# Loading a weight half ahead of the fourth head pair, and swapping a chunk of q on VectorE

## The chip, the cores and the metric

The kernel runs on one core of one Trainium2 chip. Its time is the device time of one launch in microseconds (us). The engines are TensorE (PE, with its weight loads as PEld), VectorE (DVE), ScalarE (ACT), GpSimd (POOL) and SyncE (SP), which here issues nearly all transfers.

## The reference

```python
def _attn_ref(q, k, v):                      # 4 batches, 8 heads, 576 positions, head size 64
    scores = scale * np.matmul(q, k.transpose(0, 1, 3, 2))
    gamma = 1.0 - 2.0 ** (-5.0 - np.arange(H))
    Dmat = np.where(rel >= 0, gamma[:, None, None] ** rel[None, :, :], 0.0)
    return np.matmul(scores * Dmat[None, :, :, :], v)

def _moe_ref(x, w_in, w_out):                # 2304 tokens, 512 -> 2048 -> 512
    h = x @ w_in
    g = h * np.clip(h + 3.0, 0.0, 6.0) / 6.0
    return g @ w_out

def _moe2_ref(x, w_in, w_out, g_ln):         # 512 -> 1024 -> 512
    h = x @ w_in
    solu = h * softmax(h)
    ln = (solu - mean(solu)) / np.sqrt(var(solu) + 1e-06) * g_ln
    return ln @ w_out
```

The output is `_moe2_ref(_moe_ref(_attn_ref(q, k, v)))`, with the heads of a token laid side by side as its 512 features. The inputs are float32; the weights of the two MLPs are float64, and reach the chip as pairs of 32-bit words.

## The kernel before

**Retention.** The 32 heads are taken as 16 pairs; a pair lies with one head on partitions 0 to 63 and the other on 64 to 127. The 576 positions of a pair are cut into four chunks of 128 and one of 64. Within a chunk the scores are computed and masked; what earlier chunks give is carried in a state of 64x64 per head, decayed from chunk to chunk. `attention()` (L533) is a generator with three steps for each pair `pr`. Step 0 puts out `scores(pr)`, `last_scores(pr)` and `from_states(pr - 1)`; step 1 the loads of pair `pr + 3`, `chunk_states(pr)` and `prep(pr + 1)`; step 2 `values(pr - 1)`. The matmuls of all these and most of ACT's evacuations are held in the order of the program (`keep_in_program_order`), and so are SP's weight loads. All else, VectorE's work and the loads of the pairs among it, is ordered by a planner that simulates the program.

**What an engine does for a pair.** ACT scales v by a decay (`prep`, L436, three instructions, tile `v` with two buffers), and evacuates the two score banks (`st`, L455). POOL masks the scores (L456). DVE multiplies the last chunk's scores by a mask (L501), makes the four states (`chunk_states`, L470 one copy and L476 four scaled sums, two of them on 64 partitions) and evacuates the pair's result (`xa`, L527). ACT and POOL then split `xa` into two words (L260, L261). There is one buffer each for the score banks and for `xp`, in which the result is summed, so the scores of a pair wait for `st` of the pair before, and `from_states(pr)` waits for `xa` of pair `pr - 1`.

**Why q's chunk 3 is swapped.** The fourth state lies with its heads exchanged (L468, L472), so `from_states` needs chunk 3 of q with its heads exchanged too: it reads `rq[:, S:]` (L517). The host has put that exchanged copy behind q's 576 columns in HBM (L1019). For pairs 0 to 2 (`EARLY`) the kernel loads it as a transfer of its own, behind the pair's other four (L425); for the later pairs it is part of the load of q (L417), which is then 704 columns wide.

**The weights.** The first MLP's weights are prepared beside the retention. Each half is loaded as 512 KB of raw words (`wraw`, two buffers, L119). `value` makes float32 from them with two ACT instructions (`wz` L139, `wt` L144) and two of DVE (L147, L148). `words` then splits the value into a high word (ACT, L153) and a low word (DVE or POOL, L158). In the loop at L591 the first raw half is loaded after step 2 of pair 0, the second after step 2 of pair 1. `begin` (the value) runs after step 1 of even pairs from pair 2 on, and `step` (the words) after step 2 of odd pairs from pair 3 on. From pair 4 on (`A_FROM`) each step 2 also puts out a share of the first MLP's matmuls (`mlp_h`, L272), which fill the TensorE time beside the retention.

**Transfers.** Eight semaphores take turns for SP's transfers, so that an issue waits for the landing of the transfer eight places before it.

After the retention come the rest of the first MLP (L272, L297), and the second MLP with the norm and the output (L71 in the profile, since a helper records these).

```python
        for h in range(2):
            keep(se.activation(out=st[h], in_=sp[h], func=ACTF.Copy, ...))       # L455
...
        ve.tensor_copy(out=state[:, 0], in_=up[:, 0])                            # L470
...
            (1, state[:, 0], rq[:, CHUNKS[1]]), (3, state[:, 2], rq[:, S:]),     # L517
...
        ve.tensor_tensor(out=xa, in0=xp[:, 128:704], in1=tab_sb[p], op=ALU.mult) # L527
```

Of the kernel before, what the change touches and what calls it, by code (L numbers as in the profile page):

```python
# [18 lines left out]
B, H, S, D = 4, 8, 576, 64  # L19
# [15 lines left out]
NX = 8  # L35
STEPS_B = ((6, 20, 42, 50, 58, 66), (6, 20, 42, 50, 58, 66), (4, 12, 20, 28))
W_FROM = 2
A_FROM = 4
AHEAD = 2
WRAW = 2  # L40
# [34 lines left out]
def retention_hardswish_solu_kernel(ctx, tc, kt, qt, kn, vt, w1, w2i, w2o, gln, decay, place, out):  # L75


    nc = tc.nc
    ve, se, ge, te, sy = nc.vector, nc.scalar, nc.gpsimd, nc.tensor, nc.sync
# [84 lines left out]
    def w_half(home, i, name):  # L164

        if home == "w":
            return p0.tile([128, 2, 512], F32R, tag="wi" if i == 0 else "wo", bufs=FA, name=name)
        return pb.tile([128, 2, 512], F32R, tag="wbi" if i == 0 else "wbo", bufs=4, name=name)

    def w1_halves(ffs, home, order):  # L170

        for k, i in order:
            ff = ffs[k]
            if (ff, 1 - i) not in w1t and home == "wb":
                for j in range(2):
                    w1t[ff, j] = w_half(home, j, f"w1_{ff}_{j}")

            def tile_of(ff=ff, i=i):
                if home == "w":
                    w1t[ff, i] = w_half(home, i, f"w1_{ff}_{i}")  # L180
                return w1t[ff, i]

            yield w1[ff][:, i * 1024:(i + 1) * 1024], lambda ws, raw, tile_of=tile_of: (
                ws.words(tile_of(), ws.begun.pop(), pin=True) if ws.begun else ws.words(tile_of(), ws.value(raw))
            )

    def in_first(n):
        return [(k, i) for i in range(2) for k in range(n)]

    def in_turn(n, ahead):  # L190

        return sorted(in_first(n), key=lambda ki: (ki[0] + ahead * ki[1], -ki[1]))
# [196 lines left out]
    raws, vs, sts, sts4, states, us, xps = {}, {}, {}, {}, {}, {}, {}  # L389
    HEADS, ALL = [slice(0, 64), slice(64, 128)], slice(0, 128)  # L390
    CHUNKS = [slice(128 * c, min(128 * c + 128, S)) for c in range(NV)]
# [7 lines left out]
    def mm_a(*args, **kw):  # L399
        keep(nc.tensor.matmul(*args, **kw))  # L400

    def load_pair(pr):

        if pr >= NPAIR:
            return
        early = pr < EARLY
        if early:
            tag = "wi" if pr < 2 else "g"
            rk, rq, rn = [p0.tile([128, n], F32, tag=tag, bufs=FA, name=f"raw{pr}_{i}")
                          for i, n in enumerate((S, S + 128, 512))]  # L410
        else:
            rk = pa.tile([128, S], F32, tag="rk", bufs=3, name=f"rk{pr}")
            rq = pa.tile([128, S + 128], F32, tag="rq", bufs=4, name=f"rq{pr}")
            rn = pa.tile([128, 512], F32, tag="rn", bufs=3, name=f"rn{pr}")
        nc.sync.dma_start(out=rk, in_=kt[pr])
        n = S if early else S + 128
        nc.sync.dma_start(out=rq[:, :n], in_=qt[pr][:, :n])  # L417
        if early:
            rv = p0.tile([128, 9, D], F32, tag="g", bufs=FA, name=f"rv{pr}")
        else:  # L420
            rv = pa.tile([128, 9, D], F32, tag="rv", bufs=3, name=f"rv{pr}")
        nc.sync.dma_start(out=rv, in_=vt[pr])
        nc.sync.dma_start(out=rn, in_=kn[pr])
        if early:
            nc.sync.dma_start(out=rq[:, n:], in_=qt[pr][:, n:])  # L425
        raws[pr] = rk, rq, rn.rearrange("p (c d) -> p c d", d=128), rv

    def prep(pr):
# [13 lines left out]
    def scores(pr):  # L442

        sp = [ps_a.tile([128, 512], F32, tag=f"s{h}", bufs=1, name=f"s{pr}_{h}") for h in range(2)]
        st = sts[pr] = [pa.tile([128, 512], F32, tag=f"st{h}", bufs=2, name=f"st{pr}_{h}") for h in range(2)]
        k, q, _, _ = raws[pr]
        for c in range(4):
            for o in range(2):
                for h in range(2):
                    mm_a(  # L450
                        sp[h][HEADS[o], CHUNKS[c]], k[HEADS[h], 128 * c + 64 * o:128 * c + 64 * o + 64],
                        q[HEADS[h], CHUNKS[c]], start=(c == 0), stop=(c == 3),
                    )
        for h in range(2):
            keep(se.activation(out=st[h], in_=sp[h], func=ACTF.Copy, scale=GAMMA[2 * (pr % NP) + h] ** -128))  # L455
            keep(ge.affine_select(  # L456
                out=st[h], in_=st[h], compare_op=ALU.is_ge, fill=0.0,
                base=0, pattern=[[0, 4], [1, 128]], channel_multiplier=-1,
            ))

    def chunk_states(pr):

        rn, v = raws[pr][2], vs[pr]
        up = ps_a.tile([128, 4, 64], F32, tag="u", bufs=1, name=f"u{pr}")
        state = states[pr] = pa.tile([128, 4, 64], F32, tag="state", bufs=2, name=f"state{pr}")
        for c in range(4):
            for h in range(2):
                o = HEADS[1 - h if c == 3 else h]  # L468
                mm_a(up[o, c], rn[:, c, HEADS[h]], v[:, 4 * h + c], start=(c == 0), stop=(c == 3))
        ve.tensor_copy(out=state[:, 0], in_=up[:, 0])  # L470
        for c, to, at in (
            (1, ((ALL, ALL),), H + pr % NP), (2, tuple(zip(HEADS, HEADS[::-1])), H + pr % NP),  # L472
            (3, ((ALL, ALL),), H + 2 * NP + pr % NP),
        ):
            for i, o in to:
                ve.scalar_tensor_tensor(  # L476
                    out=state[o, c], in0=state[i, c - 1], scalar=decay_sb[i, at:at + 1], in1=up[i, c],
                    op0=ALU.mult, op1=ALU.add,
                )

    def places():

        pp = mm_tile([128, NP * 128], "place")
        mm_a(pp, place_row[:, :128], place_row[:, 128:], start=True, stop=True)
        keep(se.activation(out=place_sb.rearrange("p a b -> p (a b)"), in_=pp, func=ACTF.Copy))
# [9 lines left out]
    def last_scores(pr):  # L495
        zp = ps_a.tile([128, 64], F32, tag="z", bufs=1, name=f"z{pr}")
        st4 = sts4[pr] = pa.tile([128, 64], F32, tag="st4", bufs=2, name=f"st4{pr}")
        k, q, _, _ = raws[pr]
        for h in range(2):
            mm_a(zp[HEADS[h]], k[HEADS[h], CHUNKS[4]], q[HEADS[h], CHUNKS[4]], start=True, stop=True)  # L500
        ve.tensor_tensor(out=st4, in0=zp, in1=mask4[:, pr % NP], op=ALU.mult)  # L501
# [31 lines left out]
    def attention():  # L533

        for pr in range(NPAIR + 1):
            if pr < NPAIR:
                scores(pr)
                last_scores(pr)
            if pr:
                from_states(pr - 1)  # L540
            if pr < NPAIR:
                idle_mm(N_IDLE.get(pr, 0))
                if pr == 0:
                    places()
            yield pr
            if pr < NPAIR:
                load_pair(pr + EARLY)
                chunk_states(pr)
                prep(pr + 1)
                if pr < NP:  # L550
                    widen(pr)
            yield pr
            if pr:
                values(pr - 1)
            yield pr
            if pr == 1:
                tc.keep_in_program_order(nc.sync.dma_start(out=gln_sb, in_=gln))
# [11 lines left out]
    def idle_mm(n):  # L569
        for _ in range(n):  # L570
            mm_a(warm, idle[:, :128], idle[:, 128:], start=True, stop=True)

    idle_mm(N_WARM)
    for pr in range(EARLY):
        load_pair(pr)
# [3 lines left out]
    for h in range(2):  # L579
        ge.affine_select(  # L580
            out=mask4[HEADS[h]], in_=mask4[HEADS[h]], compare_op=ALU.is_ge, fill=0.0,
# [6 lines left out]
    g = [{}, {}]  # L588
    hs = mlp_hs(0, FIRST, g[0], g_a, True)
    wq = Weights(w1_halves(FIRST, "w", in_first(FA)), True, 2)  # L590
    for s, pr in enumerate(attention()):  # L591
        if pr < W_FROM and s % 3 == 2:
            wq.load_to(pr + 1)
        if pr >= W_FROM and pr % 2 == 0 and s % 3 == 1:
            wq.begin()
        if pr > W_FROM and pr % 2 == 1 and s % 3 == 2:
            wq.step()
        if pr >= A_FROM and s % 3 == 2:
            for _ in range(2):
                next(hs, None)  # L600
# [13 lines left out]
    wq = Weights(w1_halves(FB[:4], "wb", in_turn(4, 3)), False)  # L614
# [65 lines left out]
    wq = None  # L680
    for i, j in enumerate(mlp_by_ff(4, list(range(FA)), g_a, evac_partial, ps_c, first_b, X2_LAG * NP)):
        if j == 0 and wq is None:
            wq = Weights(w1_halves(FB[4:], "w", in_turn(len(FB) - 4, 1)), False)
# [230 lines left out]
    ve, se, ge, te, sy = (Pinned(tc, e) for e in (ve, se, ge, te, sy))  # L914
# [145 lines left out]
```

## Time and profile before

| | us |
|---|---|
| median of 3 runs | 649.73 (648.87 to 650.22) |
| the profiled execution, its own time | 648.45 |
| its span | 646.7 |
| PE busy in the span | 640.3 (99%) |
| PEld | 533.3 (82%) |
| ACT | 370.7 (57%) |
| DVE | 332.5 (51%) |
| POOL | 325.3 (50%) |

The granted TensorE clock is full in all 40 slices of the span. A busy share is a mean over stages that differ; matmuls overlap their weight loads and their ends are modelled, so idle time of PE is told apart from slow work by the waits and the chain. In the rows, times are in us from the start of the span; a bracket `[0.71 <-DMA x]` tells how long the engine sat idle before the instruction, and what ended that.

### The profile page before, as it was taken

How to read it: one execution, taken by the hardware profiler on the slowest of the kernel's cores; microseconds unless marked ns; L12 is line 12 of the kernel's file. 1: busy time of each engine (PE TensorE's matmuls, PEld its weight loads, DVE VectorE, ACT ScalarE, POOL GpSimd, SP SyncE). 2: the span in 40 equal slices, each digit the busy share in tenths (PEclk: the TensorE clock that was granted, in tenths of full speed). 3: DMA queues.
4: the chain of work that ended last, by engine and by line, in shares of the span. 5: the costliest groups of instructions: out<-in, count | busy, mean ns of one | idle time of the engine just before them, and what ended most of it. 6: DMA issues, size and time to landing. Idle time of an engine off the chain costs nothing.

```text
span 646.7 us, 11131 instructions
## 1 busy us (share of the span) xinstructions
PE 640.3 (99%) x4178; PEld 533.3 (82%) x4178; DVE 332.5 (51%) x618; ACT 370.7 (57%) x653; POOL 325.3 (50%) x342
## 2 busy tenths in 40 slices
PE   8999999999999999999999999999999999999998
PEld 5788888888889888888888888889988888888887
DVE  3777635244205363253565336112688877878750
ACT  5888837464426575164366247115377768787582
POOL 4778834122312434145044024516279899999353
PEclk9999999999999999999999999999999999999999
DMA  9999416296025252557864655239695334434441
GB/s 323 392 393 378 151 54 242 94 320 218 16 68 191 62 179 90 153 172 292 289 214 152 223 181 178 94 129 367 224 254 122 81 99 111 118 81 98 75 105 67
DMA packets 80459, 114.01 MB, mean 176 GB/s; under 512 B 42642, under 2 KB 47890, under 8 KB 80404
## 3 DMA queue, kind: packets, MB, share of 16 engines
q1 hardware_dynamic: 80256, 113.27, 54.6%
q8 instruction: 33, 0.54, 0.3%
q14 instruction: 22, 0.18, 0.1%
q10 hardware_dynamic: 148, 0.02, 0.0%
HBM read 71.85 MB, written 31.98 MB: 161 GB/s over the span
## 4 chain that ended last, share of the span: by engine, by line
PE 96%; DMA 2%; ACT 1%; DVE 0%; issue 0%; SPq 0%; ACTq 0%
PE h L272 31%; PE x L297 20%; PE o L71 15%; PE h L71 13%; PE acc L297 8%; PE xp L400 3%; PE x L71 2%; PE s L400 2%; PE u L400 1%; DMA wraw<-in_w_dram 1%; DMA raw<-in_qt_dram 1%; DMA raw<-in_kn_dram 1%; DVE w L158 0%; PE z L400 0%; ACT st L455 0%
## 5 line engine op out<-in xcount | busy, mean ns | idle before, releaser
L291 POOL TENSOR_TENSOR g<-gf,g 128x512 fp32r<-128x512 f32 (+1 forms) x78 | 96.0, 1231 | 216.0 <-ACT g L290 205.0
L297 PE MATMUL x<-g,w 128*128 128x512 f32 x576 | 132.0, 389 | 0.0
L272 PE MATMUL h<-xb,w 128*128 128x512 f32 (+1 forms) x600 | 129.7, 360 | 0.2 <-DVE w L158 0.2
L297 PEld LDWEIGHTS x<-g,w 128*128 128x128 f32 x576 | 108.1, 188 | 22.4
L272 PEld LDWEIGHTS h<-xb,w 128*128 128x128 f32 x600 | 98.5, 189 | 17.9 <-issue 1.9
L285 DVE SCALAR_TENSOR_TENSOR gf<-r,h 128x512 f32<-128x512 f32 (+1 forms) x80 | 50.5, 633 | 119.9 <-ACT r L284 106.3
L71 PE MATMUL o<-w,lt 128*128 128x512 f32 (+1 forms) x456 | 103.1, 378 | 0.0
L71 PEld LDWEIGHTS o<-w,lt 128*128 128x128 f32 x456 | 82.4, 188 | 16.3 <-POOL lt L71 0.4
L284 ACT ACTIVATE r<-h,half 128x512 f32<-128x512 f32 (+1 forms) x80 | 50.7, 637 | 64.6 <-PE h L272 64.6
L272 PE MATMUL h<-xB,w 128*128 128x512 f32 x360 | 82.4, 389 | 0.0
L272 PEld LDWEIGHTS h<-xB,w 128*128 128x128 f32 x360 | 67.6, 188 | 14.0
L290 ACT ACTIVATE g<-gf 128x512 fp32r<-128x512 f32 (+1 forms) x78 | 46.1, 591 | 43.5 <-DVE gf L285 38.1
L71 POOL TENSOR_TENSOR lt<-lT,lt 128x512 fp32r<-128x512 f32 x36 | 60.9, 1708 | 13.9 <-ACT lt L71 12.7
L297 PE MATMUL acc<-g,w 128*128 128x512 f32 (+1 forms) x264 | 61.9, 361 | 0.0
L71 ACT ACTIVATE e<-h,stat 128x1024 f32<-128x1024 f32 x36 | 41.3, 1148 | 34.1 <-DVE stat L71 34.1
L147 DVE TENSOR_SCALAR wz<-wz 128x512 int32<-128x512 int32 x44 | 29.6, 672 | 48.6 <-ACT wz L139 48.6
L297 PEld LDWEIGHTS acc<-g,w 128*128 128x128 f32 x264 | 46.9, 188 | 8.8
L71 PE MATMUL h<-w2t,xt 128*128 128x512 f32 x216 | 53.5, 389 | 0.0
L71 PEld LDWEIGHTS h<-w2t,xt 128*128 128x128 f32 x216 | 40.3, 188 | 8.2
L71 PE MATMUL h<-w2b,xt 128*128 128x512 f32 x162 | 39.9, 390 | 0.1
L139 ACT ACTIVATE wz<-wraw 128x512 f32<-128x512 f32 x44 | 29.3, 665 | 18.1 <-DMA wraw<-in_w_dram 9.4
L71 PEld LDWEIGHTS h<-w2b,xt 128*128 128x128 f32 x162 | 30.1, 188 | 6.6 <-issue 0.5
(114 smaller groups left out, 839.6 us busy)
## 6 DMA issues: line engine op xcount, KB each, us to landing
wraw<-in_w_dram SPq DMA_DIRECT2D x32, 512.0 KB, 5.5
xs<-xb SPq DMA_DIRECT2D x12, 512.0 KB, 7.2
xB<-xs SPq DMA_DIRECT2D x12, 512.0 KB, 6.2
rv<-in_vt_dram SPq DMA_DIRECT2D x16, 288.0 KB, 6.0
x2l<-x2s SPq DMA_DIRECT2D x18, 256.0 KB, 4.1
x2f<-x2o SPq DMA_DIRECT2D x18, 256.0 KB, 3.6
x2r<-x2f SPq DMA_DIRECT2D x9, 512.0 KB, 3.9
rq<-in_qt_dram SPq DMA_DIRECT2D x13, 352.0 KB, 6.2
```

Source lines behind the costliest of these rows:

```text
L71: return lambda *args, **kw: self.keep(op(*args, **kw))
L139: first = se.activation(out=z.bitcast(F32), in_=raw[:, :, 1].bitcast(F32), func=ACTF.Prelu, scale=2.0 ** -112, alpha=2.0 ** 32)
L147: ve.tensor_scalar(out=z, in0=z, scalar1=3, scalar2=None, op0=ALU.logical_shift_left)
L272: mm = nc.tensor.matmul(hp, w1t[ff, 0][:, a, c], xb[t, p][:, b, :n], start=(p == 0 and i == 0), stop=(p == NP - 1 and i == 2),)
L284: se.activation(out=r, in_=hp, func=ACTF.Relu, scale=1.0 / 6.0, bias=half)
L285: ve.scalar_tensor_tensor(out=gf, in0=r, scalar=1.0, in1=hp, op0=ALU.min, op1=ALU.mult)
L290: se.activation(out=g[ff][:, 0], in_=gf, func=ACTF.Copy)
L291: ge.tensor_tensor(out=g[ff][:, 1], in0=gf, in1=f32(g[ff][:, 0]), op=ALU.subtract)
L297: te.matmul(acc, w1t[ff, 1][:, a, c], g[:, b], start=(first and i == 0), stop=(last and i == 2))
L400: keep(nc.tensor.matmul(*args, **kw))
```

## The change

The first raw weight half is issued right behind the loads of pairs 0 to 2, ahead of those of pair 3; before, it came behind them. The second raw half stays where it was (after step 2 of pair 1, which is `s == 5`).

For the first five pairs (`TURNED`) the exchanged chunk 3 is no longer loaded: the three transfers of 64 KB of pairs 0 to 2 go, and the loads of q of pairs 3 and 4 are 576 columns wide, not 704. In their place `chunk_states` copies chunk 3 of q on VectorE, each head's 64 partitions onto the other's (two `tensor_copy` of 64x128 float32). They stand in the program ahead of the pair's states.

```diff
+TURNED = 5
...
-        n = S if early else S + 128
+        n = S if pr < TURNED else S + 128
         nc.sync.dma_start(out=rq[:, :n], in_=qt[pr][:, :n])
...
         nc.sync.dma_start(out=rn, in_=kn[pr])
-        if early:
-            nc.sync.dma_start(out=rq[:, n:], in_=qt[pr][:, n:])
...
                 mm_a(up[o, c], rn[:, c, HEADS[h]], v[:, 4 * h + c], start=(c == 0), stop=(c == 3))
+        if pr < TURNED:
+            rq = raws[pr][1]
+            for h in range(2):
+                ve.tensor_copy(out=rq[HEADS[1 - h], S:], in_=rq[HEADS[h], CHUNKS[3]])
         ve.tensor_copy(out=state[:, 0], in_=up[:, 0])
...
     wq = Weights(w1_halves(FIRST, "w", in_first(FA)), True, 2)
+    wq.load_to(1)
     for s, pr in enumerate(attention()):
-        if pr < W_FROM and s % 3 == 2:
-            wq.load_to(pr + 1)
+        if s == 5:
+            wq.load_to(2)
```

## Rows read from the trace of the kernel before

**Rows 1.** Chain that ended last, 11 to 27 us: start, length, what

```profile
11.67 6.70 DMA wraw<-in_w_dram
20.35 0.97 ACT st L455 x2
21.36 0.94 PE s L400 x25
23.75 1.62 DVE w L158
25.41 1.20 PE h L272 x4
```

**Rows 2.** Busy us by stretch: PE, PEld, DVE, ACT, POOL; then clock, DMA share, GB/s

```profile
12.64:25.41 12.77, 11.02 (x268) 9.27 (x266) 8.53 (x23) 10.26 (x24) 8.56 (x13) 1.00 1.04 390
25.41:81.00 55.59, 55.59 (x1064) 44.87 (x1068) 38.40 (x105) 48.65 (x110) 44.30 (x57) 1.00 0.85 317
81.00:475.00 394.00, 393.99 (x1936) 332.88 (x1925) 161.84 (x248) 185.82 (x325) 132.66 (x118) 1.00 0.52 175
```

**Rows 3.** Waits of PE's matmuls, whole span: us in total, times, longest

```profile
PE s L400 <- ACT st L455: 1.3, 1, 1.3
PE xp L400 <- DVE xa L527: 0.2, 1, 0.2
PE h L272 <- DVE w L158: 0.2, 1, 0.2
```

**Rows 4.** Waits of PE's weight loads, whole span

```profile
PEld s L400 <- ACT st L455: 1.8, 2, 1.5
PEld h L272 <- DVE w L158: 0.6, 1, 0.6
```

**Rows 5.** Timeline of ACT, 16 to 21 us: start, length, instruction

```profile
16.52 1.15 ACT L436 ACTIVATE v<-rv,decay_sb 128x256 f32<-128x256 f32 x3 [0.71 <-DMA rv<-in_vt_dram]
18.40 0.71 ACT L139 ACTIVATE wz<-wraw 128x512 f32<-128x512 f32 x1 [0.73 <-DMA wraw<-in_w_dram]
...
19.59 0.76 ACT L260 ACTIVATE xb<-xa 128x512 fp32r<-128x512 f32 x2
20.25 1.05 ACT L455 ACTIVATE st<-s 128x512 f32<-128x512 f32 x2
```

**Rows 6.** Transfers by kind: count, KB each, median us to landing

```profile
wraw<-in_w_dram SPq DMA_DIRECT2D x32, 512.0 KB, 5.5
...
raw<-in_qt_dram SPq DMA_DIRECT2D x3, 64.0 KB, 4.7
```

**Rows 7.** Timeline of SP's issues, 17 to 19 us

```profile
17.11 0.33 SPq L415 DMA_DIRECT2D rk<-in_kt_dram  x1
18.39 0.33 SPq L417 DMA_DIRECT2D rq<-in_qt_dram  x1
```

**Rows 8.** DVE's groups to 82 us, shapes apart: count, busy us, mean ns

```profile
L476 DVE SCALAR_TENSOR_TENSOR state<-state,decay_sb,u 64x64 f32<-64x64 f32 x32 | 8.9, 280 | 0.8
...
L470 DVE COPY state<-u 128x64 f32<-128x64 f32 x16 | 3.5, 217 | 5.0 <-PE u L400 5.0
```

**Rows 9.** Waits of DVE to 82 us

```profile
DVE state L470 <- PE u L400: 5.0, 4, 1.9
```

**Rows 10.** Timeline of DVE, 19 to 24 us

```profile
19.14 0.43 DVE L147 TENSOR_SCALAR wz<-wz 128x512 int32<-128x512 int32 x1 [1.59 <-ACT wz L139]
...
21.63 0.76 DVE L527 TENSOR_TENSOR xa<-xp,tab_sb 128x576 f32<-128x576 f32 x1
...
23.75 1.61 DVE L158 TENSOR_TENSOR w<-wz,w 128x512 fp32r<-128x512 f32 x1 [0.92 <-ACT w L153]
```

**Rows 11.** Timeline of PE, from_states of pair 3

```profile
22.44 0.27 PE L400 MATMUL xp<-st,v 64*64 64x64 f32 x2
```

**Rows 12.** One line's instructions, L147, to 90 us: ns min/median/max

```profile
L147 DVE TENSOR_SCALAR wz<-wz x8: 421/427/999, 19.1 to 81.4; 128x512 int32<-128x512 int32 x8
```

**Rows 13.** The same for POOL's mask, L456, to 82 us

```profile
L456 POOL TENSOR_SCALAR_AFFINE_SELECT st<-st x32: 627/637/649, 8.0 to 77.4; 128x512 f32<-128x512 f32 x32
```

## The prediction

> **What bounds the kernel now.** I read the busy table first (PE 640.3 of 646.7 us), then the same by stretch, then PE's waits, and last the timelines of the one stretch that has idle time. By stretch [rows 2] PE is without a hole from 25.41 us on for the next 450 us; only from 12.64 to 25.41 us is it busy 11.02 of 12.77. PE's waits name the holes [rows 3]: 1.3 us before the scores of pair 4 (they wait for ACT to evacuate pair 3's), 0.2 for DVE's xa, and 0.2 before the first MLP's matmuls, for the low word of the first weight half. Since the ends of matmuls are modelled, the weight loads' waits give the upper price of the same places [rows 4]: 1.8 and 0.6. So the change, all of whose edits act before 25 us, can gain 1.7 us, at the very most about 2.6 (1.8 + 0.2 + 0.6). Whatever it does there moves the dense rest as a block.
>
> The chain that ended last says why PE waits [rows 1]: the landing of the raw weight half, then ACT's st, the scores, the low word, and from 25.41 on PE alone. ACT's timeline shows the link [rows 5]. Its order is written out: v of pair 3, wz and wt of the weight, xb, st of pair 3. It waits 0.71 us for pair 3's v, works 1.15 on it, waits 0.73 for the weight half and starts wz at 18.40; st, which PE waits for, starts at 20.25. Between 18.40 and 20.25 ACT has no wait.
>
> **The change part by part.**
>
> *The weight half ahead of pair 3.* This takes the 0.73 us wait of wz away: the half lands four transfers of pair 3 earlier, some 3 us at a rate of 390 GB/s [rows 2]. But it puts 512 KB in front of pair 3's v, for which ACT waits already. SP issues in order and the transfers are saturated in this stretch (a DMA share of 1.04), so what is put in front delays what is behind. By bytes, 524,288 at 390 GB/s is 1.34 us; SP's issues, each of which waits for an older landing, stand 1.28 apart around that half [rows 7].
>
> *The swapped chunk not loaded.* Three transfers of 64 KB [rows 6] stood ahead of pair 3's v, and pair 3's load of q was wider by the same 64 KB. Four times 65,536 bytes at 390 GB/s is 0.67 us. Between the two prices of the half, 1.31, pair 3's v lands 1.31 - 0.67 = 0.64 us later. The small transfers may cost more than their bytes; the bounds are 0.3 (each costs half as much again as its bytes: 1.28 - 4 x 0.25) and 1.34 (they cost nothing). I take 0.55, near the bytes. From pair 4 on all loads land about 0.85 us earlier (five times 64 KB), but no wait of PE from there on names a transfer, so I cost that at nothing; the cover is PE's own dense work.
>
> *Sum for ACT.* v of pair 3 starts at 16.52 + 0.55 = 17.07 and ends 1.15 later, at 18.22; wz follows at once, 0.18 before its 18.40. wt, xb and st follow unchanged, and PE's scores come 0.18 earlier, about 0.2. By the bounds: 0.3 late gives 0.43 earlier, 1.34 late gives 0.61 later. Pair 3's k and q are late by about the same 0.6 us, for scores that PE reaches at 16.17; a short wait there lies in front of the 1.3 us hole and is paid from it.
>
> *The copies.* The trace of before has no 64x128 copy from SBUF. Nearest are the 64x64 scaled sums that change partitions, 0.280 us, and the 128x64 copy, 0.217 [rows 8]. Twice the columns bounds it at 0.56 from above; 0.2 bounds it from below. I take 0.28 each, so 0.56 us a pair, and 0.4 to 1.1 as ends. They read only q, which is there before the pair's scores. For pairs 0 to 2 DVE sits idle in front of the first state until PE has made it: four such waits sum to 5.0 us, the longest 1.9 [rows 9]. The copies, which stand in the program ahead of that state, fit there and cost nothing. For pair 3 DVE idles 1.59 us until ACT's wz, and 0.92 before the low word at 23.75 [rows 10], in which pair 4's can lie. Cover gone, the price is this: DVE's xa of pair 2 ends at 22.39 (21.63 + 0.76) and PE's from_states of pair 3 starts at 22.44 [rows 10, 11], so 0.56 us behind that wait shows nearly whole, less the 0.18 that the chain has become earlier: some 0.35 a pair. I take the covered place, since the work behind which they would queue (L147) waits itself.
>
> What speaks against the copies is how DVE and POOL meet. L147, one source and one result in SBUF like them, takes 0.427 us as a rule and 0.999 at worst [rows 12], so 0.57 more. The Trainium skill has a rule for this (SBUF — State Buffer, "Who interferes with whom"): a copy on VectorE that uses both ports and a GpSimd instruction lock each other out for a whole instruction. The trace agrees as far as the 0.57 is close to one POOL mask of 0.637 [rows 13]. By the rule a copy that meets a mask costs 0.28 + 0.57 = 0.85, without it 0.28; hidden in idle time neither moves the sum. What it does where they are not hidden is a rival below.
>
> *Sum.* -0.18 from ACT; the 0.2 us wait for the low word goes along unchanged, because ACT's high word and DVE's low word move with st; copies 0. About -0.2 us: from the profiled execution's 648.45 to 648.25. Its time lies 1.3 below the median of the runs, which I take as the level to compare at: 649.73 - 0.2 = 649.5.
>
> **The rivals.**
>
> *Nothing moves.* Pair 3's v is late by as much as the weight was, 0.73 us, and the hole stays as it is. For it: one queue, saturated, in order. Against it: the saved 0.67 us. 649.7.
>
> *The hole goes.* The small transfers cost far more than their bytes, so that pair 3's v is hardly late: wz 0.7 earlier, and the low word, no longer late for PE, gives its 0.2 to 0.6 as well. Together 0.9 to 1.7, time 648.0 to 648.8. For it: chain and waits name this one transfer. Against: the 0.71 us wait for v comes first and can only grow, and ACT's work from v to st has no other slack. To pass 1.3 us, PE would have to find st ready.
>
> *The copies come into PE's path (slower).* The planner puts the copies of pairs 3 and 4 behind the weight's words, ahead of the states, and each meets a POOL instruction: two copies of 0.85 us a pair, 1.7, less 0.2 of slack, for two pairs: +3.0, less the 0.2 gained, so 652.5. It decides from the point at which a pair's copies end xa later than PE's 22.44, that is from about 0.25 us on; without meeting POOL it is 0.35 a pair, +0.5 in all, 650.2. For it: xa and PE stand 0.05 apart. Against: DVE's idle 1.59 and 0.92 us just there. The lock is the Trainium skill's rule named above, the durations are this trace's.
>
> *Another order elsewhere (slower).* The planner simulates the whole program, and the matmuls after the retention are not held. With PE full for 394 us another order there can only lose; 1.5 us as a guess of the size of the largest hole now, 651.2. Nothing in the profile points to it.
>
> **How the numbers follow.** The forecast 0.47, nothing moves 0.20, the hole goes 0.18, copies in the path 0.11, another order 0.04. A measurement of this kernel tells 0.2% from no change, that is 1.3 us. The forecast and "nothing moves" lie within it; of the hole's case I count most as faster, with some of the forecast's own upper end, 0.18. The two last cases in their full size are slower, 0.15, and the rest is 0.67. The range reaches down to the hole's case, 648.1, and up to where the copies cost about half their full price, 651.0; the likeliest case alone spans 649.1 to 650.3, its bounds for ACT.
>
> **What would show it.** In the profile after: ACT's wz right behind v with no wait for wraw; ACT's wait for pair 3's v grown from 0.71 to about 1.25; st of pair 3 starting near 20.1; PE's wait before pair 4's scores near 1.1; ten 64x128 copies of about 0.28 us in DVE's idle time. I am wrong if pair 3's v lands no later than before, if PE's waits name xa, the states or the copies between 22 and 29 us, or if idle time appears after 81 us.

## The result, and the profile after

The changed kernel takes 657.15 us in the median (656.74 to 660.19, four runs), the kernel before 649.4 beside it: 1.0128 of it, with a 95% interval of 1.0096 to 1.0161. It is slower by some 8 us, far outside the forecast range. The profiled execution takes 657.37 us with a span of 655.6; line numbers in it are from 1 lower to 4 higher. One run of a later kernel (709.35 us, at a mean granted clock of 0.85) is in a slower state and stands in no ratio below.

First the same table by stretch that showed where PE had idle time [rows 2]; columns are PE, PEld, DVE, ACT, POOL, granted clock, DMA share, GB/s. The first line is the kernel before, the others are the changed kernel:

```profile
5.12:12.64 7.52, 7.46 (x148) 5.18 (x147) 2.38 (x10) 4.71 (x11) 4.14 (x10) 1.00 1.06 389
5.12:12.64 7.52, 5.19 (x99) 3.43 (x100) 2.33 (x7) 4.82 (x11) 4.32 (x10) 1.00 1.04 374
12.64:25.41 12.77, 8.48 (x141) 6.32 (x135) 4.52 (x17) 2.62 (x7) 0.87 (x1) 0.60 0.96 356
25.41:81.00 55.59, 55.01 (x1131) 44.63 (x1127) 39.89 (x109) 49.37 (x113) 45.29 (x59) 1.00 0.87 309
81.00:475.00 394.00, 393.99 (x1999) 331.98 (x1998) 160.09 (x249) 185.72 (x329) 132.88 (x119) 1.00 0.51 174
```

The dense rest is as dense as before. The loss arises ahead of 25.41 us: PE was busy 7.46 us between 5.12 and 12.64 and is now busy 5.19; between 12.64 and 25.41 it was busy 11.02 and is now busy 8.48, at a mean clock of 0.60. PE's waits name two new places. The 1.4 us for `idle` lie ahead of all loads and are there in the kernel before too; of the waits in [rows 3] only 0.4 us for st is left:

```profile
PE xp L401 <- DVE state L479: 4.3, 1, 4.3
PE z L401 <- DVE st L504: 2.3, 1, 2.3
PE warm L401 <- DVE idle L569: 1.4, 1, 1.4
PE s L401 <- ACT st L454: 0.4, 1, 0.4
```

Both new waits are for VectorE. Its timeline from 4 to 22 us says why; L472 are the new copies, L504 the mask of the last chunk (before L501), L473 and L479 the states:

```profile
4.62 0.45 DVE L472 COPY raw<-raw 64x128 f32<-64x128 f32 x2 [3.30 <-DMA raw<-in_qt_dram]
8.21 0.94 DVE L472 COPY raw<-raw 64x128 f32<-64x128 f32 x2 [3.13 <-DMA raw<-in_qt_dram]
11.15 0.97 DVE L472 COPY raw<-raw 64x128 f32<-64x128 f32 x2 [2.01 <-DMA raw<-in_qt_dram]
12.15 0.22 DVE L504 TENSOR_TENSOR st<-z,mask 128x64 f32<-128x64 f32 x1
12.29 0.21 DVE L473 COPY state<-u 128x64 f32<-128x64 f32 x1
12.54 0.28 DVE L479 SCALAR_TENSOR_TENSOR state<-state,decay_sb,u 128x64 f32<-128x64 f32 x1
16.83 0.22 DVE L472 COPY rq<-rq 64x128 f32<-64x128 f32 x1 [4.00 <-DMA rq<-in_qt_dram]
16.97 0.58 DVE L479 SCALAR_TENSOR_TENSOR state<-state,decay_sb,u 64x64 f32<-64x64 f32 x2
17.47 0.22 DVE L472 COPY rq<-rq 64x128 f32<-64x128 f32 x1
17.73 0.28 DVE L479 SCALAR_TENSOR_TENSOR state<-state,decay_sb,u 128x64 f32<-128x64 f32 x1
19.72 0.46 DVE L472 COPY rq<-rq 64x128 f32<-64x128 f32 x2 [1.72 <-DMA rq<-in_qt_dram]
20.21 0.23 DVE L504 TENSOR_TENSOR st<-z,mask 128x64 f32<-128x64 f32 x1
```

The copies of pairs 1 and 2 stand ahead of pair 0's mask, those of pair 3 between pair 0's states, those of pair 4 ahead of pair 1's mask. VectorE works its queue off in order here. So pair 0's mask, which ran at 6.46 before, stands behind the q loads of pairs 1 and 2 (8.2 and 11.1 us) and runs at 12.15; pair 0's later states stand behind the load of pair 3 (16.8), and pair 1's mask behind that of pair 4 (19.7). The kernel before, for comparison, first on VectorE and then on PE:

```profile
6.46 0.23 DVE L501 TENSOR_TENSOR st<-z,mask 128x64 f32<-128x64 f32 x1 [5.13 <-PE z L400]
```
```profile
9.62 0.85 PE L400 MATMUL xp<-raw,state 64*64 64x128 f32 x16
12.65 1.10 PE L400 MATMUL s<-raw,raw 64*64 64x128 f32 x32
```

PE's timeline in the changed kernel, and ACT's chain once PE gets there:

```profile
9.00 1.10 PE L401 MATMUL s<-raw,raw 64*64 64x128 f32 x32
...
17.29 1.25 PE L401 MATMUL xp<-raw,state 64*64 64x128 f32 x12 [4.29 <-DVE state L479]
18.47 1.46 PE L401 MATMUL warm<-idle 128*128 128x512 bf16 x3
19.86 1.12 PE L401 MATMUL u<-v,raw 128*64 128x64 f32 x16
20.77 1.92 PE L401 MATMUL xp<-st,v 128*64 128x128 f32 x16
22.63 1.31 PE L401 MATMUL s<-raw,raw 64*64 64x128 f32 x32
```
```profile
26.08 1.15 ACT L435 ACTIVATE v<-rv,decay_sb 128x256 f32<-128x256 f32 x3 [0.51 <-ACT st L454]
27.13 0.76 ACT L140 ACTIVATE wz<-wraw 128x512 f32<-128x512 f32 x1
```

The scores of pair 1 start at 9.00 (before 8.61), those of pair 2 at 22.63 (12.65), of pair 3 at 25.91 (16.17), of pair 4 at 29.68 (20.88). The delay is 0.4 us at pair 1, grows by 9.6 between pairs 1 and 2, and falls by 1.2 to 8.8 at pair 4, where most of PE's wait for st is gone: ACT no longer waits for the two transfers of [rows 5], since by 26 us both have landed. The 0.4 is within the scatter from one execution to the next: the same kernel run again has pair 1's scores at 8.30. Of the 9.6, 6.6 are PE's two waits (7.3 by its weight loads, 2.6 and 4.7). From the end of the second wait, inside from_states of pair 0, to the scores of pair 2 PE takes 5.3 us; the whole of from_states and the rest took 3.0 before (9.62 to 12.65). Behind the waits PE runs at the lower of its two levels, 1.2 GHz. The granted clock by stretch (same columns as above):

```profile
12.00:17.00 5.00, 0.57 (x12) 0.33 (x12) 0.93 (x6) 0.00 (x0) 0.60 (x2) 0.59 1.02 371
17.00:22.00 5.00, 4.71 (x43) 3.29 (x45) 2.48 (x12) 0.00 (x0) 0.00 (x0) 0.50 1.03 386
```

### The profile page after: what moved, and what is told of

Read it like the earlier page. It is cut to its first block, busy times and chain, and to the rows that moved or that the text cites. A ratio compares the mean times of both kernels' runs of the same rounds, so it can differ in the third digit from the quotient of the medians.

```text
span 655.6 us, 11134 instructions
## 1 busy us (share of the span) xinstructions
PE 643.6 (98%) x4178; PEld 535.2 (82%) x4178; DVE 336.2 (51%) x628; ACT 371.0 (57%) x653; POOL 325.6 (50%) x342
## 4 chain that ended last, share of the span: by engine, by line
PE 96%; DMA 2%; ACT 0%; SPq 0%; DVE 0%; issue 0%
PE h L273 31%; PE x L298 20%; PE o L72 15%; PE h L72 13%; PE acc L298 8%; PE xp L401 3%; PE s L401 2%; PE x L72 2%; PE u L401 1%; DMA rq<-in_qt_dram 1%; DMA rv<-in_vt_dram 1%; DVE w L159 0%; PE warm L401 0%; PE z L401 0%; ACT st L454 0%; SPq L418 0%
## 5 line engine op out<-in xcount | busy, mean ns | idle before, releaser
L291 ACT ACTIVATE g<-gf 128x512 fp32r<-128x512 f32 (+1 forms) x78 | 46.1, 591 | 43.2 <-DVE gf L286 38.2
L148 DVE TENSOR_SCALAR wz<-wz 128x512 int32<-128x512 int32 x44 | 29.7, 675 | 47.7 <-ACT wz L140 47.6
L262 POOL TENSOR_TENSOR xb<-xa,xb 128x512 fp32r<-128x512 f32 (+7 forms) x32 | 28.6, 913 | 23.0 <-ACT xb L261 22.8
```

Of the source, the lines that this page charges most:

```text
L148: ve.tensor_scalar(out=z, in0=z, scalar1=3, scalar2=None, op0=ALU.logical_shift_left)
L262: ge.tensor_tensor(out=x[:, 1, c], in0=src, in1=f32(x[:, 0, c]), op=ALU.subtract)
L291: se.activation(out=g[ff][:, 0], in_=gf, func=ACTF.Copy)
```

## The experiments

Three theories stood: "order" (the place of the copies in VectorE's queue), "loads" (the weight half in front of pair 3) and "copies" (their own length, or what they lose beside POOL). Ratios are to the kernel before on the same chip, with 95% intervals.

**The change, held.** Mask, copies and first state copy are held in the order of the program:

```diff
-        ve.tensor_tensor(out=st4, in0=zp, in1=mask4[:, pr % NP], op=ALU.mult)
+        keep(ve.tensor_tensor(out=st4, in0=zp, in1=mask4[:, pr % NP], op=ALU.mult))
...
-                ve.tensor_copy(out=rq[HEADS[1 - h], S:], in_=rq[HEADS[h], CHUNKS[3]])
+                keep(ve.tensor_copy(out=rq[HEADS[1 - h], S:], in_=rq[HEADS[h], CHUNKS[3]]))
-        ve.tensor_copy(out=state[:, 0], in_=up[:, 0])
+        keep(ve.tensor_copy(out=state[:, 0], in_=up[:, 0]))
```

> The change whole, with VectorE's mask of the last chunk, its copies of q and its first state copy held in the order of the program, so that a pair's copies stand right ahead of that pair's state. Theory 'order' (the planner moved the copies of pairs 1 to 4 ahead of pair 0's mask and states, and VectorE's queue, which goes in order, waited there for loads still on their way): the waits of PE for the mask (2.3 us) and the state (4.3 us) go, and the time is that of the kernel before less 0.2 us, 649.2 (648.6 to 649.8). Theory 'loads' (the weight half in front of pair 3's loads is what costs): still 655 to 657. Theory 'copies' (the copies cost by their own length or by meeting POOL): 652 to 656.

Measured 651.21, ratio 1.0028 (1.0019 to 1.0037). About three quarters of the loss go by the order alone, which speaks against "loads" as the main cause. But 1.9 us stay, which "order" did not expect. PE's waits in this kernel, and the copies of pair 3 in VectorE's and POOL's timelines:

```profile
PE xp L401 <- DVE xa L530: 1.4, 2, 1.2
PE warm L401 <- DVE idle L569: 1.4, 1, 1.4
PE s L401 <- ACT st L454: 0.9, 1, 0.9
```
```profile
20.95 1.34 DVE L472 COPY rq<-rq 64x128 f32<-64x128 f32 x2
22.21 0.21 DVE L473 COPY state<-u 128x64 f32<-128x64 f32 x1
22.45 0.89 DVE L479 SCALAR_TENSOR_TENSOR state<-state,decay_sb,u 128x64 f32<-128x64 f32 x3
23.38 0.76 DVE L530 TENSOR_TENSOR xa<-xp,tab_sb 128x576 f32<-128x576 f32 x1
```
```profile
20.66 1.54 POOL L262 TENSOR_TENSOR xb<-xa,xb 128x512 fp32r<-128x512 f32 x2 [1.76 <-ACT xb L261]
```

Pair 3's two copies take 1.34 us beside POOL's split. They stand behind the weight's value (L148, L149) and ahead of pair 3's states, and xa, for which PE waits 1.2 us, stands behind them. This is the first of the forecast's two slower rivals, close to the place named there. Behind that wait PE's clock falls in this execution, too:

```profile
22.00:25.00 3.00, 1.77 (x54) 1.64 (x46) 2.19 (x8) 1.56 (x6) 2.06 (x5) 0.79 0.99 375
```

So part of what is left may be the clock's; the copies alone, held, below lose nearly as much at full clock.

**The control**, the kernel before with its mask and first state copy held (the same diff without the copies).

> A control: the kernel before, with the same VectorE instructions held in the order of the program, which is the order they had. All theories: 649.4, no difference beyond 0.1%. If it differs, holding them has a price of its own that has to be taken off the other held kernels.

649.42, ratio 0.9997 (0.9986 to 1.0008). Holding has no measurable cost.

**The weight half early, alone** (`wq.load_to(1)` ahead of the loop; no copies, all loads as before).

> The weight half ahead of pair 3's loads alone; q's chunk 3 is loaded as before, nothing is copied. Theory 'order': pair 3's v lands 1.3 us later and the weight half no longer is waited for; ACT's st of pair 3 starts 0.6 us later, so +0.6: 650.0 (649.5 to 650.6). Theory 'loads': most of the loss, 654 to 657. Theory 'copies': as 'order'.

649.98, ratio 1.0010 (1.0000 to 1.0019): 0.7 us for the 0.6 expected. This is the direct evidence against "loads". ACT's timeline shows the exchange of waits; compare [rows 5]:

```profile
17.86 1.15 ACT L436 ACTIVATE v<-rv,decay_sb 128x256 f32<-128x256 f32 x3 [1.58 <-DMA rv<-in_vt_dram]
18.92 0.68 ACT L139 ACTIVATE wz<-wraw 128x512 f32<-128x512 f32 x1
```

**The copies alone, held and not held** (the loop's loads of the weights as before; the held one with the first diff).

> The copies alone, held in the order of the program; the weight half is loaded behind pair 3 as before. Theory 'order': the loads land 0.6 to 0.85 us earlier, ACT's v of pair 3 starts at 16.3, the weight half lands near 17.5, st of pair 3 starts near 19.4 in place of 20.25, so -0.9: 648.5 (648.0 to 649.2), a little faster than the held whole. Theory 'copies': 652 or more. Theory 'loads': 649.4 or faster.

> The copies alone and not held; the weight half is loaded behind pair 3 as before. Theory 'order': the planner again puts the copies of pairs 1 to 3 ahead of pair 0's state, and those of pair 4 ahead of pair 1's mask; PE's from_states of pair 0 waits for pair 3's q (landing near 15 us), and pair 4's q near 19 holds pair 1's mask; about as slow as the change whole, 656 (654.5 to 658). Theory 'loads': 649, since the weight half is back in its place. Theory 'copies': 652 to 656, with VectorE busy and not waiting for loads.

Held 650.88, 1.0023 (1.0014 to 1.0032); not held 655.94, 1.0107 (1.0090 to 1.0124). The second confirms "order" with the weight half in its old place. The first missed its 648.5: st of pair 3 came at 19.59 (0.66 earlier than before; 0.9 was expected), but PE then waited 1.23 and 0.94 us for xa of pairs 2 and 3, behind 1.34 and 1.27 us of copies. The granted clock of its profiled execution is full throughout:

```profile
PE xp L401 <- DVE xa L530: 2.4, 3, 1.2
```

**Copies for three pairs only**, not held and held.

```diff
-TURNED = 5
+TURNED = 3
```

> The change with TURNED = 3: copies for pairs 0 to 2 only, not held; pairs 3 and 4 load the swapped chunk with q. Theory 'order': VectorE's queue now waits at most for pair 2's q, which landed at 11.15 us; pair 0's state comes near 12.5 in place of 8.6, and since ACT's later waits absorb about a microsecond the loss is 2 to 3.5 us: 652 (651 to 653). Theory 'copies' (cost by number): six copies of ten, so about 60% of the loss, 654. Theory 'loads': 657, as the weight half stays early.

> Copies for pairs 0 to 2 only, held in the order of the program, and the weight half early: the kernel with TURNED = 3 that was not held (653.17), with nothing but VectorE's order changed. Theory 'order': its whole loss goes, 649.3 (648.8 to 649.9). Theory 'copies meet POOL' (what is left of the loss when all ten are held, 1.9 us, comes from the copies of pairs 3 and 4, which took 1.27 and 1.34 us beside POOL's split and mask and held back xa): also 649.3, as these two pairs load their chunk again. If held copies cost wherever they stand: 650.4, three fifths of 1.9.

Not held 653.17, 1.0056 (1.0041 to 1.0071): a little under half the loss, just above the 651 to 653 that the landing of pair 2's q foretold. PE waits 2.8 us for pair 0's mask here and not at all for its state. Held 650.32, 1.0018 (1.0008 to 1.0028), and 0.4% is won by the order. But 649.3 was expected, and 650.32 is what held copies would give if they cost wherever they stand (650.4). No wait for xa is left in its trace (0.2 us, as before), so pairs 3 and 4 are where copies meet POOL on the path. Some of the remaining 0.18% may be the early half's 0.10%; the intervals don't tell them apart. The next kernel, with the same six copies, speaks against a price of copies as such.

**Three pairs held, the half in its old place**:

> The same with the weight half behind pair 3 as before: only the three small transfers are gone, against six copies in VectorE's idle time. By 'order' and 'copies meet POOL': loads land 0.6 us earlier from pair 3 on, the weight half near 17.7, st of pair 3 near 19.6, so 0.5 us faster than the kernel before: 648.8 (648.2 to 649.4). If held copies cost wherever they stand: 650.4.

649.44, 1.0004 (0.9994 to 1.0015), no measurable difference; a gain of 0.5 us was expected. In its trace st of pair 3 starts at 19.81 (before 20.25), and the scores of pair 5 at 26.09 (26.54), as expected; by pair 7 they start at 36.13 (35.87), and PE's matmuls list no wait in between. Two groups of matmuls take longer than in the kernel before: from_states of pair 5 0.95 us for 0.62 (at 27.13), the values before pair 7's scores 1.41 for 1.05 (at 33.20). In both PE's weight loads pause, 0.36 and 0.29 us, for nothing that the profile shows. Groups longer than usual stand in other traces as well (1.26 us for 1.05 in that of the early half alone). What brings the pauses about is open, and whether the other executions lose the 0.5 us in this way is not shown.

**All ten copies, placed elsewhere**: behind xa of two pairs before and ahead of the pair's own mask, held there (`swap_q` holds the copies' lines; pair 0's stand ahead of its own states). Mask and first state copy are held as above.

```diff
             if pr:
                 values(pr - 1)
+            if pr < NPAIR - 1:
+                swap_q(pr + 1)
             yield pr
```

> All ten copies, but those of a pair stand right behind xa of two pairs before, ahead of the pair's own mask, and the weight half is loaded behind pair 3 as before. VectorE's queue is then idle where they stand (pair 3's ahead of the weight's words, pair 4's ahead of its low word), and no load is late there. 'Copies meet POOL': the wait for xa (1.23 and 0.94 us in the kernel with the copies alone, held) goes; 648.7 (648.2 to 649.6), with up to 0.5 lost where pair 4's copies meet POOL's mask and hold back pair 3's last state. If held copies cost wherever they stand: 651.

> The same placing with the weight half early, so the change whole with all its loads, and only the copies elsewhere. 'Order' and 'copies meet POOL': 649.3 (648.7 to 650.0), as first forecast for the change, and up to 0.6 us behind the same placing with the weight half in its old place, since pair 3's v comes later. If the weight half early cost something that no run has shown so far: 651 or more.

With the half in its old place 649.68, 1.0010 (1.0002 to 1.0019), 1 us more than expected; with it early, so the change whole, 649.53, 1.0009 (1.0000 to 1.0018), as expected. Placing and holding ten copies turns +1.3% into +0.1%, and holding alone had no cost in the control. The wait for xa falls to 0.2 us in both. Of the waits left, one is for pair 3's last state, behind the copies of pair 4, as expected in kind (early half):

```profile
PE s L401 <- issue: 0.7, 2, 0.5
PE xp L401 <- DVE state L475: 0.7, 2, 0.5
PE s L401 <- ACT st L454: 0.6, 1, 0.6
PE xp L401 <- DVE xa L533: 0.2, 1, 0.2
```

No version is measurably faster than the kernel before.

**The clock.** PE's two waits filled with idle matmuls, 31 (10 and 21, as below) and then 26 (9 and 17), since the 31 outlasted the second wait:

```diff
                 scores(pr)
+                if pr == 1:
+                    idle_mm(10)
                 last_scores(pr)
...
                 mm_a(xp[HEADS[h], at_x(c)], w[r], q[r], start=(c == 1), stop=False)
+            if pr == 0 and c == 1:
+                idle_mm(21)
```

> The change whole, with 31 idle matmuls more on PE (10 behind the scores of pair 1, 21 after the first matmuls of from_states of pair 0), about as long as PE's two waits there; their product is not used. If part of the loss is the clock's lower level, which the profile shows from about 12 to 22 us, it stays at the upper level now and PE's work from the end of the wait to the scores of pair 2 takes 3.0 us as in the kernel before, not 5.3: about 2.3 us faster than the change, 654.9 (654 to 655.8). If the waits alone are the loss, no faster than the change, 657.

> As the filled kernel before (656.98, no faster than the change), but with 26 idle matmuls in place of 31, since those outlasted PE's second wait: from_states of pair 0 went on at 17.99 us, while its state was there at 17.6. If the clock's lower level is part of the loss: PE's work from there to the scores of pair 2 takes 2.7 us in place of 5.3, pair 5's scores start 1.5 to 2.5 us earlier than the change's 35.33, and the time is 1.5 to 2.5 us below the change's run beside it. If what the clock gives is given back behind it (ACT's chain from v of pair 2 to st of pair 3, which cannot start before PE's values of pair 0, and the loads): within 0.7 us of the change.

> The change itself once more, beside the filled kernel on one chip: 657.2 (656.4 to 658.0) by every theory, and the half clock from about 12 to 22 us again in its records if the two long waits bring it about.

31: 656.98, 1.0117 (1.0102 to 1.0132). 26: 656.5, 1.0112 (1.0094 to 1.0129), beside the change again at 657.08, 1.0123 (1.0103 to 1.0143). The clock stayed at its upper level in both filled kernels; the stretch from 17 to 22 us with 26, and in the change run again:

```profile
17.00:22.00 5.00, 4.26 (x89) 3.13 (x92) 3.06 (x13) 1.28 (x4) 0.00 (x0) 1.00 1.05 394
```
```profile
17.00:22.00 5.00, 4.59 (x50) 3.34 (x55) 2.46 (x11) 0.00 (x0) 0.00 (x0) 0.58 1.05 395
```

With 26 PE takes 2.9 us from the end of its second wait to the scores of pair 2 (17.16 to 20.09), in the change beside it 4.8 (17.08 to 21.85). Of this gain of 1.8 us, 1.1 is left at pair 5 (33.34 for 34.46), and the span is 1.3 us shorter, 654.0 for 655.3. Most of the rest is lost where PE at the upper clock runs into a new wait for xa of pair 0, since VectorE's states, late by pair 4's copies, now come last:

```profile
21.89 0.27 PE L401 MATMUL xp<-st,v 64*64 64x64 f32 x2 [0.58 <-DVE xa L532]
```

In the times the difference is 0.6 us, and the intervals allow anything from nothing to over 2. So the clock's share is not told from zero in the times, and is some 1 us of 8 in this one pair of traces. Either way it comes behind the two waits, which bring the lower level about: filled, they leave the clock at its upper one.

## Why the prediction was wrong

**The step that failed** is the sentence on the copies of pairs 0 to 2, "The copies, which stand in the program ahead of that state, fit there and cost nothing", with the one ahead of it, "They read only q, which is there before the pair's scores". Both hold for a queue in the program's order. VectorE's instructions here are ordered by the planner, and copies that read nothing but a load may go ahead of any pair's work. The planner put them up to three pairs ahead (pair 3's among pair 0's states), where q was not there: PE waited 2.3 and 4.3 us, and held in order the same change loses 1.9 us in place of 8. The idle time that I counted as cover (5.0 us, [rows 9]) was that of a queue with no such instruction in it. Since nothing bound the copies to their pair, the price had to be bounded by the landing of the latest q in front of the earliest work that could stand behind it, not by the length of a copy: 19.7 us for pair 4's, against 6.46 for pair 0's mask. Even in the program's order the step fails for pairs 3 and 4: "I take the covered place" put pair 3's copies into VectorE's 1.59 us of idle time ahead of L147, and in the held kernel they run behind it, at 20.95, in front of xa.

**The rivals.** "The copies come into PE's path" named the right engine and the right object, with a wrong place (behind the weight's words) and a wrong price, 3.0 us from the copies' length beside POOL. In the change as it is, waits for loads set the price, and "another order elsewhere" was thought of only for work behind the retention. Once the copies are held in order, the rival is what is left, with its place and its size about right: copies of 1.34 and 1.27 us a pair for the 1.7 worked out, 1.9 us lost for 2.8 (1.6 with the loads as before).

**What held.** The bound on any gain and the dense rest that moves as a block. The exchange of ACT's waits: with the half early alone, v comes later, the wait for the weight is gone, and PE waits 0.4 us for pair 3's q; by the prediction's terms (1.31 - 0.73) that is +0.6, and +0.7 was measured. The loads' price by bytes is not shown: with three and with all five chunks not loaded st of pair 3 starts 0.44 and 0.66 us earlier, about as worked out, but in the control, which has the loads of the kernel before, it starts at 20.73, 0.48 later than there. The sum itself, for the work in the place that it assumed, was -0.2 us; with the copies placed elsewhere the change measures +0.6 (0.0 to 1.2), so even there the sign is not confirmed.

**Sizes.** A copy alone takes 0.22 us, not 0.28. Beside POOL single copies take up to 1.05, more than the 0.85 worked out. The 0.57 in that price was read as a POOL mask of 0.637, but the L147 of 0.999 us in the kernel before (81.44 to 82.43) ran beside another POOL instruction, L291, which took 1.28 us and ended at 82.16; that 0.57 is near a mask's length was chance. In the held kernel, one line's instructions with min, median and max ns:

```profile
L472 DVE COPY raw<-raw x6: 221/223/558, 7.5 to 15.3; 64x128 f32<-64x128 f32 x6
L472 DVE COPY rq<-rq x4: 269/628/1054, 20.9 to 27.6; 64x128 f32<-64x128 f32 x4
```

Five of these ten take longer than 0.23 us, and each of the five ends 0.08 us behind the end of a POOL instruction. The longest runs from 20.95 to 22.00, beside a split that takes 1.27 us and ends at 21.93. That agrees with the Trainium skill (SBUF — State Buffer, "Who interferes with whom"), by which a copy on VectorE that uses both ports and a GpSimd instruction exclude each other for a whole instruction. So what a copy loses is what is left of the POOL instruction that it meets, and a split of 1.27 us leaves more than a mask.

## What to carry to other kernels

An instruction whose only input is a load is free to move in a program that a planner orders, and in a queue that is worked off in order, as VectorE's was here, it makes all behind it wait for that load. Before counting idle time as its cover, ask what holds it there; if nothing does, price it by the landing of its input at the earliest place it can take, or bind it. Small work added to VectorE belongs behind what PE waits for: placed behind xa, pair 4's copies still take 1.22 us beside POOL's masks, but the wait for xa is gone, and a wait of 0.5 us for pair 3's last state takes its place.

## What was not expected of the hardware

The lower clock level behind PE's two waits (a mean of 0.54 of the full clock from 12 to 22 us) made PE's own work there 2.3 us longer, but cost less than that: some 1 us of 8 by the pair of traces with and without it, 0.6 in the times and not told from zero. Part of that time VectorE's chain would have held PE anyway, 0.6 us of 1.8 in that pair.

A short VectorE copy beside POOL ends with POOL's instruction (0.08 us behind it, five times in the held kernel), so 0.22 us can become 1.05.
